# Score matmuls moved from 32x32 to 64x32 array tiles, and a new order of all pieces, in a one-core attention and feed-forward kernel

## The chip, the cores and the metric

The kernel runs on one core of one Trainium2 chip. A core has five engines that run their own instruction queues in order and meet at semaphores: TensorE (PE in the profile, with its weight loads on a row of their own, PEld), VectorE (DVE), ScalarE (ACT), GpSimd (POOL) and SyncE (SP), which only issues DMAs. The metric is device time in microseconds. Three runs of the kernel before gave a median of 218.65 us (218.47 to 218.85).

## The reference, cut to what matters

Inputs are x, 8 batches by 8 heads by 512 tokens by 64, and state, 8 by 8 by 32 by 64. Each head reads both ways; the heads are then joined and go through a two-layer network.

```python
scores = scale * np.matmul(x, state.transpose(0, 1, 3, 2))      # 512 x 32 a head
a = softmax(scores);   xread = np.matmul(a, state)              # 512 x 64
scores2 = scale * np.matmul(state, x.transpose(0, 1, 3, 2))     # the same products, turned
a2 = softmax(scores2); sread = np.matmul(a2, x)                 # 32 x 64
h = concat([xread, sread], tokens), heads side by side          # 8 * 544 rows of 512
r = np.maximum(h @ w_in, 0.0)                                   # 512 -> 2048
out = (s * r * r + b) @ w_out                                   # 2048 -> 512
```

## The kernel before, in words

The whole program is a list of named pieces, ORDER (L15). The loop at L724 takes it word by word and emits each piece's instructions, so ORDER fixes the order in every engine's queue, DMA issues included. It says nothing about how pieces of different engines line up in time: that is left to the semaphores. A piece on another engine, or a load, starts as soon as its own queue and its data allow. The first number in a name is the batch, and a last letter A, V or G puts the piece on ACT, DVE or POOL.

For one batch b the pieces are, in the order of the data:

- x.b (L177) loads x, converted to fp16, by two DMAs that POOL issues. From batch 3 on, POOL first makes a tiny copy that waits for the transposed x of the batch before. xn.b (L188) loads x in another layout by four POOL DMAs; it has two buffers. For batch 0 there are x0.0 and x0.1 and two copies castx.
- xT.b (DVE, L286) transposes x in 32x32 blocks. casts, pair and turn prepare the states: pair.i0.i1 (L255) block-transposes the states i0 to i1 of 16 on DVE, and turn (L243) transposes them on PE, four or fewer at a time, and copies them to the tile stT.
- T.b (PE, L294) makes the scores of all 8 heads: for each of two halves e of the 64 features, four positions hp and two groups g, one matmul of 32 rows by 32 columns of weights and 512 moving columns, 16 in all. U, mu, D, E1, z, At and A (DVE, ACT, POOL) are the softmax over the states, and A holds its result for PE. keep.b (ACT, L309) copies the scores out of PSUM for batches 0, 1, 2 and 7.
- nm, nms, E2, a2, aps, a2T are the other softmax, V.b.c (PE, L403) the read by it for two batches at a time, srd.b (ACT, L423) its copy to srdT.
- M.b.j (PE, L426) multiplies the states by a quarter of w_in: 8 matmuls in tiles of 64 rows by 32 columns. Mc.b.j copies the result to fp16. So xread @ w_in is formed as A @ (state @ w_in), with 256 instead of 512 rows to sum over.
- l.b.f (L378) is that product for one of 16 blocks of 128 features of the first layer: 2 matmuls on PE, a relu on ACT. s.b.f.n squares n blocks. Batches 0 to 2 then use L.b.rr.q (L401), 4 matmuls of the second layer each, and out (DVE) with stores from SP; lh and sh are half-width forms for batch 0. Batches 3 to 7 use seven products in place of eight: S forms sums of blocks, P.b.u is half a product (8 matmuls), ev (L600) evicts a PSUM bank on DVE, and put stores. wsum forms the matching sums of w_out.
- lsr, ssr, S_sr, P_sr, ev_sr do the same for the 256 rows of sread at the end.
- idle.n (L668) issues n matmuls on ones.

PSUM tiles have few buffers: own=1 pieces of T and M share one (tag pt), own=0 pieces share another (pa), l and lh have two (ph), L, P and idle have two (po). A piece that takes a buffer waits for the last reader of the piece that had it.

The 16 matmuls of T run at array positions (row 32 r, column 32 hp) with r = hp ^ g (L300). M uses rows 64 g, and V all 128 rows with 64 columns. All three share that heads of a group stand in the order r = hp ^ g in the column blocks.

Of the kernel before, what the change touches and what calls it, by code (L numbers as in the profile page):

```python
# [78 lines left out]
def kernel(  # L79
# [21 lines left out]
    P = 128  # L101
# [116 lines left out]
    nc.scalar.dma_start(sb_one[:, 0:1], moe_s.unsqueeze(0))  # L218
    nc.scalar.dma_start(sb_one[:, 1:2], moe_b.unsqueeze(0))
    nc.vector.memset(ones16, 1.0)  # L220
    nc.vector.memset(ones32, 1.0)
    xh_t[0] = xpool.tile([P, NG, NT, D], FP16, name="xh_0", tag="xh")

    def load_first_x(g):
# [533 lines left out]
```

## Time and profile before

| what | value |
|---|---|
| median of 3 runs | 218.65 us |
| the profiled execution itself | 218.68 us, span 216.8 us |
| PE busy | 207.0 us, 1920 matmuls |
| DVE busy | 169.4 us |
| ACT busy | 154.7 us |
| POOL busy | 105.0 us |
| granted TensorE clock, mean | 0.998 |

The span is the time from the first to the last instruction of the program; 1.9 us of the execution lie outside it. Busy shares are averages: matmuls overlap, so the start of one piece to the start of the next is the better measure of what a piece costs PE, and it is the one used below. On other engines an instruction's time overlaps a little with the one behind it: relus of 0.60 us follow each other every 0.50 us. In the timeline a row is a run of like instructions with its start, the time from its first start to its last end, and in brackets what the engine waited for.

### The profile page before, as it was taken

The numbers are of one execution on the slowest core, as the hardware profiler recorded it, in microseconds if no ns is written. First come the engines' busy times: TensorE is split into PE (matmuls) and PEld (weight loads), VectorE is DVE, ScalarE is ACT, GpSimd is POOL, SyncE is SP. The second block draws the span as 40 slices with busy tenths as digits, with TensorE's granted clock in tenths as the row PEclk, the third lists the DMA queues.
The fourth block names the chain that finished last, engine by engine and source line by source line (L and its number), as shares of the span: only waits on it lengthen the run. The fifth ranks groups of instructions, "written<-read, shape, count | busy, mean of one in ns | idle before, by whom it ended". The sixth has DMA issues, their size and how long they took to land.

```text
span 216.8 us, 4729 instructions
## 1 busy us (share of the span) xinstructions
PE 207.0 (95%) x1920; PEld 126.4 (58%) x1920; DVE 169.4 (78%) x236; ACT 154.7 (71%) x262; POOL 105.0 (48%) x102
## 2 busy tenths in 40 slices
PE   7668999999999999999999999999999999999992
PEld 2334444344444434545677666776667777888881
DVE  2699885989867879986998799979887964785571
ACT  4378987898858788899889899667668866444400
POOL 8529123494679930525254318836564334225330
PEclk9999999999999999999999999999999999999999
DMA  6999992759497262192908850718903600450055
GB/s 153 186 205 205 199 197 42 125 124 133 106 173 120 48 99 49 38 155 55 144 9 137 139 110 4 97 39 139 205 10 65 131 0 3 87 111 0 0 153 141
DMA packets 23657, 22.42 MB, mean 103 GB/s; under 512 B 4436, under 2 KB 17492, under 8 KB 23636
## 3 DMA queue, kind: packets, MB, share of 16 engines
q0 software_dynamic: 16848, 12.52, 40.8%
q1 hardware_dynamic: 5504, 8.66, 16.4%
q10 hardware_dynamic: 1284, 0.95, 1.6%
q8 instruction: 15, 0.25, 0.5%
q14 instruction: 6, 0.05, 0.1%
HBM read 25.72 MB, written 8.91 MB: 160 GB/s over the span
## 4 chain that ended last, share of the span: by engine, by line
PE 90%; ACT 5%; DMA 2%; DVE 0%; issue 0%; SPq 0%
PE hps L461 24%; PE ops L505 19%; PE opf_X L137 16%; PE opf_W L137 8%; PE mps L137 4%; PE opf_Y L137 4%; PE hps_sr L461 3%; PE vps L137 2%; DMA xf<-in_x_dram 2%; ACT M L152 2%; PE aps L137 2%; PE ops_sr_X L137 2%; PE T_None L137 2%; ACT rh L491 1%; PE dps L672 1%; PE hph L137 1%
## 5 line engine op out<-in xcount | busy, mean ns | idle before, releaser
L465 ACT ACTIVATE r<-hps 128x512 f16<-128x512 f32 x120 | 67.5, 602 | 27.8 <-PE hps L461 26.3
L461 PE MATMUL hps<-A,M 128*128 128x512 f16 x240 | 64.7, 380 | 0.0
L137 PEld LDWEIGHTS <-g 128*128 128x128 f16 x480 | 46.6, 98 | 11.4 <-issue 0.7
L505 PE MATMUL ops<-w_out,g 128*128 128x512 f16 x192 | 46.3, 379 | 0.0
L471 POOL TENSOR_TENSOR g<-r 128x1024 f16<-128x1024 f16 (+1 forms) x14 | 30.4, 2180 | 23.7 <-ACT r L465 23.7
L461 PEld LDWEIGHTS <-M 128*128 128x128 f16 x240 | 21.7, 98 | 22.7 <-issue 6.2
L505 PEld LDWEIGHTS <-g 128*128 128x128 f16 x192 | 18.7, 98 | 22.2 <-issue 0.4
L152 ACT CAST M<-mps 128x1024 f16<-128x1024 f32 x22 | 22.3, 1017 | 1.6 <-PE mps L137 1.5
L469 ACT ACTIVATE g<-r 128x1024 f16<-128x1024 f16 (+1 forms) x18 | 21.4, 1210 | 0.1
L192 POOL DMA_DIRECT2D xn<-in_x_dram x32 | 18.6, 592 | 5.6 <-PE vps L137 4.9
L346 POOL TENSOR_TENSOR At<-E,rz 128x1024 f16<-128x1024 f16 x5 | 9.8, 1964 | 22.0 <-ACT r L465 11.3
L137 PE MATMUL opf_X<-w_T,g 128*128 128x256 f16 x160 | 19.8, 272 | 0.0
L575 DVE TENSOR_TENSOR g<-g 128x1024 f16<-128x1024 f16 (+1 forms) x20 | 17.9, 908 | 1.1 <-POOL S L575 0.9
L575 POOL TENSOR_TENSOR g<-g 128x1024 f16<-128x1024 f16 x4 | 8.8, 2207 | 19.6 <-PE opf_X L137 12.4
L471 DVE TENSOR_TENSOR g<-r 128x1024 f16<-128x1024 f16 (+1 forms) x18 | 14.7, 836 | 1.6 <-ACT r L465 1.6
L152 DVE CAST M<-mps 128x1024 f16<-128x1024 f32 x10 | 12.1, 1213 | 3.5 <-PE mps L137 3.0
L604 DVE SCALAR_TENSOR_TENSOR osx<-opf_X,sb_bc,bias_bc 128x512 f32<-128x512 f32 x15 | 11.2, 746 | 4.0 <-PE opf_X L137 3.9
L292 DVE STREAM_TRANSPOSE xT<-xh 128x1024 f32<-128x1024 f32 (+2 forms) x12 | 10.4, 869 | 4.7 <-ACT xh L152 4.1
L325 POOL TENSOR_TENSOR Dm<-U,mu 128x1024 f32<-128x1024 f32 x3 | 5.7, 1913 | 15.0 <-DVE mu L321 15.0
L465 ACT ACTIVATE r_sr<-hps_sr 128x256 f16<-128x256 f32 x16 | 6.1, 382 | 7.9 <-PE hps_sr L461 7.2
L137 PE MATMUL mps<-w_in,stT 64*32 64x512 f16 x256 | 11.2, 383 | 0.3
L515 DVE SCALAR_TENSOR_TENSOR osb<-ops,sb_bc,bias_bc 128x512 f32<-128x512 f32 x12 | 8.8, 737 | 3.4 <-PE ops L505 3.4
(101 smaller groups left out, 324.3 us busy)
## 6 DMA issues: line engine op xcount, KB each, us to landing
out_dram<-osx SPq DMA_DIRECT2D x36, 128.0 KB, 2.4
xn<-in_x_dram POOLq DMA_DIRECT2D x32, 128.0 KB, 5.1
xh<-in_x_dram POOLq DMA_DIRECT2D x14, 256.0 KB, 5.1
w_in<-in_moe_w_in_dram POOLq DMA_DIRECT2D x8, 256.0 KB, 8.3
w_out<-in_moe_w_out_dram POOLq DMA_DIRECT2D x4, 512.0 KB, 11.2
out_dram<-osb SPq DMA_DIRECT2D x16, 128.0 KB, 2.6
out_dram<-osb SPq DMA_DIRECT2D x16, 64.0 KB, 4.4
xf<-in_x_dram SPq DMA_DIRECT2D x2, 256.0 KB, 3.7
```

The lines of the kernel that those rows point to most:

```text
L137: return nc.tensor.matmul(out, lhsT, rhs, start=start, stop=stop, tile_position=tp, is_transpose=is_transpose, skip_group_check=skip,)
L152: (engine.copy if engine is nc.scalar else engine.tensor_copy)(out, in_)
L192: nc.gpsimd.dma_start(out=xn_t[b][32 * jh : 32 * jh + 32].rearrange("t h c d -> t h (c d)"), in_=x[b].rearrange("h (t jh c) d -> jh t h (c ...
L292: nc.vector.transpose(part(out, p, g), part(in_, p, g))
L346: e.tensor_tensor(out, E1, over_n(rz), ALU.mult)
L461: nc.tensor.matmul(hps, lhsT, rhs, start=(i == 0), stop=(i == len(terms) - 1))
L465: nc.scalar.activation(R_t[tag, q][:, i], hps, AF.Relu)
L469: nc.scalar.activation(g, r, AF.Square)
L471: e.tensor_mul(g, r, r)
L505: nc.tensor.matmul(ops_t[tag, rr], G_t[tag][:, f, P * rr : P * rr + P], w_out_f(f), start=(f == 0), stop=(f == NKF - 1),)
L575: e.tensor_tensor(out, x, y, op)
L604: nc.vector.scalar_tensor_tensor(out, fast(b, name[0]), s_bc, out if plus else bias, ALU.mult, ALU.add)
```

## The change

The scores are now computed in tiles of 64 rows by 32 columns. Each matmul sees the transposed x of two heads at once. For that the transposed states are stored twice, in stZ[0] and stZ[1], with the rows of every other head set to zero: pair first transposes into stZ[0], then multiplies it on DVE by a column of zeros and ones, own, into stZ[1] and, in place, into stZ[0]. The column own is set by five memsets at the start. The count of matmuls stays 16 a batch. The order of heads becomes r = hp ^ 2g in T, V and M alike.

ORDER is new as a whole. It has the same pieces but for these: idle.12, idle.12 and idle.5 become idle.12, idle.11 and idle.4; many squares, sums and copies change engine or are split otherwise; and places differ, of POOL's loads too, in which x.2 now stands behind two squares on POOL. SP's stores keep their kinds, and the last two stores of batch 7 stand between the two of sread.

```diff
 ORDER = [
-    "x0.1 x0.0 castx.1.A xT.0.1.0 casts.A idle.12 pair.0.4 castx.0.A xT.0.0.0 T.0.1.0 U.0.0 turn.0.4.A "
-    "mu.0.0 D.0.V.0 E1.0.0 sb idle.12 keep.0.0 xT.0.1.1 win.0 M.1.0.0 M.0.0.1 x.1 z.0.0 xT.0.0.1 At.0.V.0 "
-    "A.0.0 win.1 wout.0 T.0.0.1 U.0.1 Mc.1.0.A mu.0.1 D.0.V.1 Mc.0.0.A lh.0.2.0 xT.1.1 lh.0.0.0 keep.0.1 "
-    "xT.1.0 idle.5 E1.0.1 win.2 M.0.1.0 T.1.1 sh.0.0.0.V Mc.0.1.A z.0.1 At.0.V.1 A.0.1 lh.0.6.0 lh.0.4.0 "
-    "keep.1 sh.0.6.0.V sh.0.4.0.V sh.0.2.0.G L.0.1.0 lh.0.0.1 lh.0.4.1 lh.0.2.1 M.0.2.0 Mc.0.2.A lh.0.6.1 "
...
-    "l.1.0 l.1.5 pair.4.16 xT.2 sh.0.4.1.V x.3 L.0.1.3 l.1.3 turn.4.12.V out.0.0 out.0.1 l.1.1 T.2.1 U.2 "
-    "M.2.3.0 Mc.2.3.A mu.2 D.2.V l.1.9 L.0.3.0 keep.2 l.1.8 l.1.7 xT.3 s.1.8.2.A L.0.2.0 M.2.1.1 "
...
+    "x0.1 idle.12 castx.1.A casts.A pair.0.4 xT.0.1.0 castx.0.A xT.0.0.0 xT.0.1.1 T.0.1.0 turn.0.4.A "
+    "U.0.0 mu.0.0 keep.0.0 x0.0 D.0.V.0 sb E1.0.0 idle.11 z.0.0 At.0.V.0 win.0 M.1.0.0 xT.0.0.1 M.0.0.1 "
+    "x.1 T.0.0.1 A.0.0 Mc.1.0.A Mc.0.0.A lh.0.2.0 U.0.1 mu.0.1 win.1 keep.0.1 wout.0 xT.1.1 win.2 D.0.V.1 "
+    "lh.0.0.0 sh.0.0.0.G win.3 xT.1.0 idle.4 E1.0.1 z.0.1 M.0.1.0 Mc.0.1.A T.1.1 lh.0.6.0 keep.1 lh.0.4.0 "
+    "At.0.V.1 A.0.1 lh.0.4.1 wout.1 sh.0.2.0.V L.0.1.0 lh.0.0.1 lh.0.2.1 M.0.2.1 Mc.0.2.A lh.0.6.1 "
+    "L.0.0.0 l.0.10 l.0.8 M.1.2.1 Mc.1.2.A sh.0.6.0.V M.0.3.0 l.0.9 l.0.11 M.1.1.1 U.1 mu.1 D.1.V wout.2 "
+    "Mc.0.3.V E1.1 M.1.3.0 sh.0.4.0.G Mc.1.3.V wout.3 l.0.12 l.0.15 L.0.0.1 s.0.10.2.A L.0.1.1 z.1 At.1.V "
+    "st l.0.14 l.0.13 s.0.8.2.G L.0.0.2 Mc.1.1.A L.0.1.2 A.1 s.0.14.2.V s.0.12.2.A sh.0.4.1.G l.1.2 "
+    "l.1.11 cps.0 cps.1 cps.2 cps.3 sh.0.2.1.V sh.0.0.1.V l.1.5 c l.1.10 L.0.0.3 pair.4.16 bias l.1.1 "
+    "l.1.6 L.0.1.3 x.2 xT.2 out.0.1 l.1.9 turn.4.12.V",
+    "l.1.0 s.1.0.2.V T.2.1 keep.2 M.2.3.0 Mc.2.3.A l.1.7 l.1.3 s.1.2.2.A L.0.3.0 sh.0.6.1.V U.2 L.0.3.1 "
...
+    "L.0.2.1 L.0.2.2 l.1.15 l.1.4 s.1.4.2.G M.2.0.0 Mc.2.1.V z.2 At.2.V A.2 T.3.1 U.3 s.1.8.4.A Mc.2.0.A "
+    "l.1.12 L.0.3.3 out.0.3 l.2.4 nm.3 L.0.2.3 L.1.0.0 out.0.2 nms.3.A mu.3 l.2.7 l.2.15 E2.3.0 s.1.6.2.G "
...
+    "l.7.0 S.6.4.0.V put.5.1.1 S.6.4.1.V P.6.6 l.7.8 s.7.6.2.V P.6.7 a2.1 l.7.14 l.7.3 aps.1 a2T.1.A "
+    "ev.6.X2 P.6.8 s.7.12.4.A ev.6.W1 P.6.9 l.7.10 l.7.11 P.6.10 ev.6.X3 s.7.10.2.V V.7.1 srd.7 srd.1 "
+    "l.7.9 s.7.8.2.V P.6.12 lsr.1",
...
 ]
...
-    stE = konst.tile([P, NR, Ns, 2], FP16, name="stE")
+    stZ = [konst.tile([P, NR, Ns, 2], FP16, name=f"stZ_{k}") for k in range(2)]
+    own = konst.tile([P, 2], FP32, name="own")
...
+    nc.vector.memset(own, 0.0)
+    for r in range(4):
+        nc.vector.memset(own[Ns * r : Ns * r + Ns, r % 2 : r % 2 + 1], 1.0)
...
     def pair_states(i0, i1):
         nc.vector.transpose(
-            stE[:, i0:i1].rearrange("p i n e -> p (i n e)").bitcast(FP32),
+            stZ[0][:, i0:i1].rearrange("p i n e -> p (i n e)").bitcast(FP32),
             stn[:, i0:i1].rearrange("p i d -> p (i d)").bitcast(FP32),
         )
+        for k in (1, 0):
+            nc.vector.tensor_scalar(stZ[k][:, i0:i1], stZ[0][:, i0:i1], own[:, k : k + 1], None, ALU.mult)
...
                 for g in range(NG):
-                    r = hp ^ g
+                    r = hp ^ 2 * g
+                    rows = slice(64 * (r // 2), 64 * (r // 2) + 64)
                     mm(
                         part(T[Ns * hp : Ns * hp + Ns], p, g)[:, 0, :],
-                        stE[32 * r : 32 * r + 32, NG * b + g, :, e],
-                        part(at[b]["xT"][32 * r : 32 * r + 32, :, :, e], p, g)[:, 0, :],
+                        stZ[r % 2][rows, NG * b + g, :, e],
+                        part(at[b]["xT"][rows, :, :, e], p, g)[:, 0, :],
                         start=(e == 0), stop=(e == 1),
-                        tp=(32 * r, Ns * hp),
+                        tp=(64 * (r // 2), Ns * hp),
                     )
...
-                    hp = k ^ g
+                    hp = k ^ 2 * g
...
-                r = hp ^ g
+                r = hp ^ 2 * g
```

95 rows, old and new, of the table ORDER are left out of this document.

## The prediction

> **What bounds the kernel now.** I read the page first, then the chain that ended last, then PE's timeline, piece by piece. From the page:
>
> ```profile
> span 216.8 us, 4729 instructions
> PE 207.0 (95%) x1920; PEld 126.4 (58%) x1920; DVE 169.4 (78%) x236; ACT 154.7 (71%) x262; POOL 105.0 (48%) x102
> PE   7668999999999999999999999999999999999992
> PE 90%; ACT 5%; DMA 2%; DVE 0%; issue 0%; SPq 0%
> ```
>
> PE is the bound from the fifth slice on (each is 5.4 us). I laid the starts of PE's pieces against the usual step of their kind (0.43 us for l, 0.86 for L, 0.87 for P). After 25.8 us nothing exceeds it by more than 0.01 us, but for one thing: ahead of every group of tiled matmuls a piece is 0.09 us longer, and the last piece of the group is about 0.11 longer. So behind 26 us the kernel has no waits to win back, only that 0.2 us at each change of tiling. It can lose, wherever the new order makes PE wait. Two stretches of PE's timeline show a change of tiling:
>
> ```profile
> 48.80 0.59 PE L461 MATMUL hps<-A,M 128*128 128x512 f16 x2
> 49.33 0.64 PE L137 MATMUL T_None<-xT,stE 32*32 32x512 f16 x16
> 49.90 0.41 PE L137 MATMUL mps<-w_in,stT 64*32 64x512 f16 x8
> ...
> 63.53 0.62 PE L137 MATMUL mps<-w_in,stT 64*32 64x512 f16 x16
> 64.09 0.39 PE L461 MATMUL hps<-A,M 128*128 128x512 f16 x1
> ```
>
> The reader is to see: T (16 matmuls of 32x32 tiles) takes 49.33 to 49.90 = 0.57 us though M of another tiling follows at once; M behind it takes to 50.25 (where the next piece starts), 0.35. Two pieces of M, 16 matmuls in one tiling, take 63.53 to 64.09 = 0.56; the second starts 0.22 or 0.23 after the first, and then 0.33 to its end. So 8 matmuls in 8 tiles cost 0.226 inside a group and 0.33 as its end.
>
> The start is another matter. This is the chain over it:
>
> ```profile
> 8.25 2.70 PE dps L672 x12
> 10.95 0.39 PE mps L137 x8
> 11.36 1.94 ACT M L152 x2
> ...
> 15.08 0.49 ACT Ts L313
> 15.56 0.04 issue
> 15.61 0.50 PE mps L137 x8
> 16.10 0.02 issue
> 16.13 1.02 ACT M L152
> 17.15 0.05 issue
> 17.19 0.62 PE hph L137 x4
> 17.82 0.02 issue
> 17.84 1.09 ACT rh L491 x2
> 18.93 0.74 ACT Ts L313
> ```
>
> Here ACT sets the pace, with PE's filler matmuls ahead. Two loads stand close behind: w_in's second quarter was issued at 4.85 and 5.53 and landed 9.3 and 10.1 us later, the last at 15.63, just as M.0.1.0 starts (15.61); the fourth quarter, issued at 15.93 and 16.6, landed by 23.8, and M.0.3.0 starts at 24.08.
>
> **Changes of tiling (PE).** T.2 and T.5 stand ahead of an M piece in the new order, T.3 and T.6 behind one, T.4 and T.7 alone; the old order pairs the same pieces. If the 16 matmuls of T fill eight 64x32 tiles like two M pieces, T inside a group costs 2 x 0.226 = 0.45 and a pair 0.45 + 0.33 = 0.78, where the trace has 0.57 + 0.35 = 0.92: -0.13 each. Alone it is 0.56 against 0.575: -0.02. T.3, T.5, T.6: -0.39; T.4, T.7: -0.04; T.2 is counted below. The old T already has four row tiles writing one bank and runs eight wide (16 in 0.57), so I take the new one to run eight wide too. Ends: no faster than M (0.56 for 16), and at worst 0.43 more each, if the two row halves cannot write one bank together (M never asks that: each half writes its own bank).
>
> The Trainium skill's page TensorEngine Tiling (Array Packing), section Restrictions and Gotchas, says that different row tiles cannot access one PSUM bank at a time. The trace of before speaks against it: by that rule the old T, with four row tiles in each bank, would take about four times 0.43 us, and 16 took 0.57. By the rule the sum would end as in the first rival.
>
> **Extra DVE work.** Five memsets lie in DVE's idle 3.0 us before its first transpose. Two multiplications of 128x256 and two of 128x768 are new. Nearest row: the 128x512 multiplication by a column in a2 took 0.363 us. In proportion 0.2 and 0.5 each; the upper bound, from the 128x512 product in At at 0.67, is 0.34 and 1.0. The first pair lies before 6.28, where DVE waits for castx.0: pair.0.4 from 4.87 ends at 5.55 (upper 5.8), xT.0.1.0 then takes 0.45, and xT.0.0.0 still starts at 6.28. Nothing, with 0.0 to 0.3 us of cover left. The second pair stands ahead of bias and xT.2. Its cost is in the next part.
>
> **The start, walked through the new queues with the old rows.** Idle.11 in place of 12 lets M.1.0.0 start at 10.66, 0.22 earlier (its weights landed at 10.56). M.0.1.0 gives that back: its load lands at 15.63. xT.1.1 now stands ahead of D.0.1, so E1.0.1 starts at 15.5 and Mc.0.1 at 16.15 (old 16.13). Behind it ACT's order changes: relu 17.86, keep.1 18.35, two relus from 19.27 and 19.77, then 20.53, 21.03, Mc.0.2 at 21.53 (old 21.71), relus 22.44, 23.24, 23.75, Mc.1.2 at 24.24 (old 24.50). U.1 must be through before M.0.2.1; it now follows two squares and keep.1 and ends at 20.65, before PE wants it (20.85). So -0.26 at this point. POOL issues w_in's last quarter 0.8 us later, behind a square that waits for a later relu, w_out's last quarter 2.5 us and st 2.5 us later; all queue behind transfers that land at 21.2 (w_in), 29.06 (w_out) and 31.55, so I cost that at nothing. If w_in's last quarter lands as much later as it is issued later, M.0.3.0 starts at 24.6, and the 0.26 turns into a loss of 0.5.
>
> At 31 to 38 us x.2 matters: issued at 20.75 before, at about 29.0 now, behind s.0.8.2.G and sh.0.4.1.G. Before it landed at 34.0 and 35.5, behind w_out and st; x's loads took 3.7 to 14.0 us, median 5.2. From its second issue at 29.6 that median gives 34.8. DVE wants it after c (33.95), pair (0.57 + 2 x 0.5, to 35.45) and bias (36.1): xT.2 ends at 37.3, T.2.1 starts at 37.86 (old 38.15). Out.0.1 and turn follow on DVE to 38.35, so M.2.3.0 starts at 38.4, held by 0.1, old 38.73: -0.33, T.2's gain included. At DVE's upper bound xT.2 ends at 38.4 and the gain is lost: +0.6.
>
> **The rest.** The same count of matmuls in the same kinds follows. Waits that I find with no cover: L.1.0.0 behind out.0.3 (U.3 now stands ahead of it on DVE) and P.5.4 behind ev.5.X1 (now behind z.7), both within 0.1 us of holding PE; +0.1 together. And the sread: V.7.1 was 4.7 us ahead of the first lsr, now l.7.9 and P.6.12 alone (1.3 us) are between them, while ACT makes two copies srd, which took 0.73 us each here, about 0.63 apart: +0.17. xn.1 is issued behind S.6.2.1.G at about 172 to 175; xn took at most 6.9 us, and V.7.1 needs it at 182: nothing. DVE, ACT and POOL have, by the rows of their pieces, about +1.5, -5 and +8 us in all, and POOL has room (48%). The last stores: SP's put of batch 7 stands between the two of sread and is issued 0.6 us before the last: nothing, at most 0.6 if SP is late.
>
> **Sum.** 218.68 (span 216.8 + 1.9 around it, 0.03 above the median) - 0.33 - 0.39 - 0.04 + 0.17 + 0.1 = 218.2.
>
> **Rivals.**
> *Row halves take turns in a bank.* In each pass the first four positions write bank by half, the second four the other way round, so every pass falls in two: +0.43 us for each of six T on a busy PE: 218.2 + 2.6 = 220.8. Against: the old T. For: no row has 64-row tiles sharing a bank.
> *x.2 lands late.* For: it is issued 8 us later, and in the busy stretch w_in's loads took 8.3 us in the median. Then it lands at 37.9, xT.2 ends at 39.1, T.2.1 is held by 1.3 us: 219.5. It is slower than before from a landing after 37.1 on, by over 0.2% after 37.6. Against: it waited only for what lies ahead of it.
> *The start gives nothing and re-ordered producers hold PE here and there.* DVE's margins at many evictions are 0.1 to 0.8 us by my walk, over stretches of DVE work with an error of a few tenths. Without the -0.33 and with three holds of 0.2: 219.1.
> *The tiling does not save.* The cost at a change may lie with leaving the full array alone; then T saves nothing: 218.2 + 0.5 = 218.7.
>
> **Chances.** Forecast 0.47 (own range 217.8 to 218.6); bank 0.07; late load 0.10; scattered holds 0.24; no saving 0.12. I call within 0.2% (0.44 us) no change, about what a measurement here can tell. Faster is the forecast's better side and little else: 0.42. Within: its other part, no saving, half of the scattered holds: 0.31. Slower: 0.27. The range 217.7 to 219.6 leaves out the bank and a tail of the holds.
>
> **What would show it.** T rows 64*32 with x16 and the next M piece 0.45 us behind (right), or 0.9 (bank). M.2.3.0 at 38.4; DVE idle before xT.2 for the load xh would mean a late load. A gap of 0.2 us ahead of the first hps_sr matmul. No PE step more than 0.1 us over its kind elsewhere; any such step names the producer that I mis-timed. The prediction is wrong if PE waits over 0.5 us in any one place after 26 us, or if M.0.3.0 starts after 24.1.

## The result, and the profile after

The changed kernel takes 221.22 us (median of 4 runs, 220.9 to 221.63) against 218.65: a ratio of 1.0112, 95% interval 1.0095 to 1.0129. The forecast was 218.2 in a range of 217.7 to 219.6. It was wrong in sign and outside its range.

The profiled execution is one of 220.9 us with a span of 218.4, against 218.68 and 216.8. Its page, the lines that answer to those of before:

```profile
span 218.4 us, 4742 instructions
PE 208.0 (95%) x1918; PEld 126.0 (58%) x1918; DVE 172.2 (79%) x250; ACT 151.0 (69%) x255; POOL 117.2 (54%) x105
PE   7868999999999999999999999999999999998992
PE 76%; DMA 9%; DVE 6%; POOL 2%; ACT 2%; issue 2%; SPq 1%; DVEq 0%; ACTq 0%; POOLq 0%
```

The first lines of such a page hide the loss: PE's busy share is the same 95%. The last line shows it. The chain that ended last was 90% PE before; now it is 76%, and DMA and DVE carry 15%, so PE waits for loads or stores somewhere. Part of that is the start, where the order is new; part lies behind 26 us, where there was nothing but PE before.

Laid against the usual step of their kind, PE's pieces between 36 us and the last product give this account:

| place | us |
|---|---|
| M.2.3.0 starts at 38.47 instead of 38.73 | -0.26 |
| changes of tiling, T.3 to T.7 | -0.36 |
| L.0.3.3 and L.0.2.3 longer by 0.17 and 0.46 | +0.62 |
| V.7.1 and P.6.12 longer by 0.08 and 0.15 | +0.23 |
| lsr.14 and lsr.15 longer by 0.86 and 0.44 | +1.29 |
| sum | +1.52 |
| P_sr.6 starts at 213.10 instead of 211.62 | +1.48 |
| from there to the end of the execution, 7.80 instead of 7.06 | +0.74 |

So 1.48 + 0.74 = 2.22 = 220.9 - 218.68; 0.04 is left between the pieces.

**The tiles.** PE's timeline over T.3:

```profile
47.77 0.41 PE L137 MATMUL mps<-w_in,stT 64*32 64x512 f16 x8
47.99 0.63 PE L137 MATMUL T_None<-xT,stZ 64*32 64x512 f16 x16
48.56 0.60 PE L468 MATMUL hps<-A,M 128*128 128x512 f16 x2
...
51.79 1.02 PE L512 MATMUL ops<-w_out,g 128*128 128x512 f16 x4 [0.29 <-DVE osb L522]
```

M and T now share a tiling: T starts 0.22 behind M and takes 0.57 as the end of the group. T.2 and T.5, which stand ahead of M, take 0.464. A pair of T and M so takes 0.79 where it took 0.92: 0.12 less for T.3, T.5 and T.6, and nothing for T.4 and T.7, which stand alone. The last line is L.1.0.0, which the profile shows as held by DVE; more on it below.

**The largest loss.** The chain over 189 to 199 us, in order of time:

```profile
188.40 0.89 PE opf_W L137 x8
189.31 0.76 DVE osx L611
190.09 0.53 SPq L620
...
191.65 0.58 SPq L620
192.28 3.68 DMA out_dram<-osx
196.24 0.57 issue
197.14 0.55 DVE g L582
198.69 0.60 PE hps_sr L468 x4
```

It leaves PE at 189.3 and comes back at 198.7. P.6.11 (188.40) completes bank W of batch 6; ev.6.W2 evicts it into osx (189.31); SP issues the stores of that tile (190.09 to 192.2); the last lands 3.7 us later, at 196.0; and only then DVE goes on. DVE's and ACT's timelines say who waits:

```profile
189.31 0.75 DVE L611 SCALAR_TENSOR_TENSOR osx<-opf_W,sb_bc,osx 128x512 f32<-128x512 f32 x1 [0.99 <-PE opf_W L137]
192.58 2.01 DVE L582 TENSOR_TENSOR g<-g 128x2048 f16<-128x2048 f16 x2
196.14 0.75 DVE L611 SCALAR_TENSOR_TENSOR osx<-opf_X,sb_bc,bias_bc 128x512 f32<-128x512 f32 x1 [1.55 <-DMA out_dram<-osx]
196.81 0.42 DVE L478 TENSOR_TENSOR g_sr<-r_sr 128x512 f16<-128x512 f16 x1
```

```profile
198.26 0.66 ACT L472 ACTIVATE r_sr<-hps_sr 128x256 f16<-128x256 f32 x2 [2.02 <-DVE g_sr L478]
```

The eviction at 196.14 is ev.7.X1, the first of batch 7. It writes the same tile osx, of which there is one buffer, so it waits for the store of the batch before. It holds DVE for 1.55 us, and the squares ssr behind it start late. They are the readers of r_sr, so ACT's relus of the sread find no buffer (2.02), and PE's lsr matmuls find no PSUM. In the kernel before, ev.6.W2 was done at 185.94 and ev.7.X1 started at 193.48, 7.5 us later, with no wait for a store (the 2.04 us of the last line come up again further down):

```profile
185.19 0.75 DVE L604 SCALAR_TENSOR_TENSOR osx<-opf_W,sb_bc,osx 128x512 f32<-128x512 f32 x1
...
193.48 0.75 DVE L604 SCALAR_TENSOR_TENSOR osx<-opf_X,sb_bc,bias_bc 128x512 f32<-128x512 f32 x1 [0.63 <-PE opf_X L137]
194.15 2.04 DVE L575 TENSOR_TENSOR g<-g 128x1024 f16<-128x1024 f16 x1
```

From the eviction's end to the last landing its stores took 4.6 us; now they took 5.9, and in the new order ev.7.X1 is ready 4.5 us behind the eviction.

The 1.3 us between 4.6 and 5.9 are one late store. Of the four stores of that tile the first three land 2.3 to 2.5 us behind their issue, the fourth 3.68; in the kernel before all four take 2.3 to 2.4. In the trace a 16 KB packet of an instruction queue runs from 193.67 to 194.81, within the fourth store's time, and the slowest of the store's own packets start one behind another from 194.81 on, as it ends. In the four profiles, here and below, in which these stores follow lsr.7, the fourth takes 3.4 to 4.1 us with such a packet in its time; in the nine others it takes 2.4, with none. With the usual 4.6 us ev.7.X1 would have waited about 0.25 us, not 1.55 (an estimate from these numbers). So the new place took away 3 us of margin and put the last store beside that packet.

**The second loss.** DVE's timeline, and POOL's, around the load of x.3, and the chain through it ("issue" is time for which the profile shows no cause):

```profile
44.00 1.25 DVE L298 STREAM_TRANSPOSE xT<-xh 128x1024 f32<-128x1024 f32 x1 [1.07 <-DMA xh<-in_x_dram]
...
49.89 1.21 DVE L324 STREAM_TRANSPOSE U<-T_None 128x1024 f32<-128x1024 f32 x1
51.02 0.71 DVE L522 SCALAR_TENSOR_TENSOR osb<-ops,sb_bc,bias_bc 128x512 f32<-128x512 f32 x1
```

```profile
37.23 0.17 POOL L181 COPY ahead<-xT 1x2 f16<-1x2 f16 x1 [7.32 <-DVE xT L298]
37.46 1.06 POOL L184 DMA_DIRECT2D xh<-in_x_dram  x2
```

```profile
37.98 5.49 DMA xh<-in_x_dram
43.47 0.03 issue
43.50 0.05 DVEq L298
43.55 0.45 issue
44.00 1.25 DVE xT L298
```

The tiny copy ahead of x.3 waits for xT.2, so x.3 is issued at 37.46 and 37.98, and its second half lands at 43.47. DVE sees that at 43.55 and starts xT.3 only at 44.00. In all, xT.3 (44.00) starts 1.07 after DVE was free for it; all of DVE behind it, A.2, U.3 and out.0.3, is that much later, and out.0.3 (51.02) frees the PSUM buffer that L.1.0.0 needs. DVE had about 0.5 us of margin there, not 1.07. The 0.45 us between the end of the wait and xT.3 stand in all eight profiles with the new tiles in which DVE waits for x.3; in the three with the old tiles (the kernel before among them) they are 0.04 to 0.05. Why is open.

### The profile page after: what moved, and what is told of

Its sections match the earlier page's. It is cut to its first block, busy times and chain, and to the rows that moved or that the text cites. A ratio compares the mean times of both kernels' runs of the same rounds, so it can differ in the third digit from the quotient of the medians.

```text
span 218.4 us, 4742 instructions
## 1 busy us (share of the span) xinstructions
PE 208.0 (95%) x1918; PEld 126.0 (58%) x1918; DVE 172.2 (79%) x250; ACT 151.0 (69%) x255; POOL 117.2 (54%) x105
## 4 chain that ended last, share of the span: by engine, by line
PE 76%; DMA 9%; DVE 6%; POOL 2%; ACT 2%; issue 2%; SPq 1%; DVEq 0%; ACTq 0%; POOLq 0%
PE hps L468 21%; PE ops L512 15%; PE opf_X L137 15%; PE opf_W L137 8%; DMA w_in<-in_moe_w_in_dram 5%; PE mps L137 3%; PE opf_Y L137 3%; DMA xh<-in_x_dram 3%; PE vps L137 2%; DMA out_dram<-osx 2%; PE aps L137 2%; PE ops_sr_X L137 2%; PE hps_sr L468 2%; PE hph L137 1%; DVE xT L298 1%
## 5 line engine op out<-in xcount | busy, mean ns | idle before, releaser
L468 PE MATMUL hps<-A,M 128*128 128x512 f16 x240 | 65.9, 380 | 0.0
L478 POOL TENSOR_TENSOR g<-r 128x1024 f16<-128x1024 f16 (+1 forms) x8 | 21.5, 2690 | 17.8 <-ACT r L472 17.8
L582 POOL TENSOR_TENSOR g<-g 128x1024 f16<-128x1024 f16 (+1 forms) x9 | 22.8, 2530 | 9.3 <-PE hps L468 4.0
L152 ACT CAST M<-mps 128x1024 f16<-128x1024 f32 x26 | 26.6, 1041 | 1.2 <-PE mps L137 1.2
L478 DVE TENSOR_TENSOR g<-r 128x1024 f16<-128x1024 f16 (+1 forms) x25 | 22.6, 919 | 4.8 <-ACT r L472 4.8
L476 ACT ACTIVATE g<-r 128x1024 f16<-128x1024 f16 (+1 forms) x13 | 18.1, 1395 | 0.1
L332 POOL TENSOR_TENSOR Dm<-U,mu 128x1024 f32<-128x1024 f32 x4 | 9.5, 2364 | 11.4 <-DVE mu L328 8.4
L582 DVE TENSOR_TENSOR g<-g 128x1024 f16<-128x1024 f16 (+1 forms) x17 | 14.8, 883 | 0.1
L353 POOL TENSOR_TENSOR At<-E,rz 128x1024 f16<-128x1024 f16 x3 | 5.7, 1913 | 14.5 <-DVE rz L344 8.1
L641 POOL TENSOR_TENSOR g_sr<-g_sr 128x512 f16<-128x512 f16 (+1 forms) x3 | 4.4, 1477 | 14.1 <-DVE g_sr L478 9.4
```

The lines of the kernel that those rows point to most:

```text
L152: (engine.copy if engine is nc.scalar else engine.tensor_copy)(out, in_)
L332: e.tensor_tensor(blk(part(Dm, p)), blk(part(at[b]["U"], p)), over_n(part(at[b]["mu"], p)), ALU.subtract)
L468: nc.tensor.matmul(hps, lhsT, rhs, start=(i == 0), stop=(i == len(terms) - 1))
L476: nc.scalar.activation(g, r, AF.Square)
L478: e.tensor_mul(g, r, r)
L582: e.tensor_tensor(out, x, y, op)
```

## Experiments

Executions of the new order fall into two groups some 5 to 7 us apart, with a few in between, by a mechanism that the second experiment shows; ratios are those of the lower group, where both occur. "The kernel before" was run beside each: 218.81 and 218.63 us (29 runs each) on the chips of the first eight kernels, 218.88 (35 runs) on that of the last four.

### The tiles alone

The changed code with the order of before.

```diff
 # after.py
-ORDER = [ ... order of after.py ... ]
+ORDER = [ ... order of before.py ... ]
```

> The new score tiles and the doubled states, in the old order of pieces. Theory 1 (the loss comes from the order: three places where PE is held, 0.53 us at 49 to 52, 0.23 at V.7.1, 1.29 at 195 to 199, while the tiles save 0.1 to 0.13 for each T): the two multiplications stand before xT.2 in the old order, so T.2.1 starts about 0.6 later than 38.15, and the T pieces give back 0.5: 218.4 to 219.1. Rival (the doubled states or the tiles themselves cost, in PE or outside the span): 220.5 to 221.5.

Measured: 219.91 us (219.1 to 220.8, 12 runs), ratio 1.0052 (1.0031 to 1.0073). Slower, not faster. The expected hold at T.2.1 is there, but it sets off another. DVE's and PE's lines, with T.2.1 at 38.76 and l.2.6 at 52.43:

```profile
36.67 0.88 DVE L265 TENSOR_SCALAR stZ<-stZ,own 128x768 f16<-128x768 f16 x2
```

```profile
38.76 0.65 PE L137 MATMUL T_None<-xT,stZ 64*32 64x512 f16 x16 [0.52 <-DVE xT L298]
...
52.43 1.04 PE L468 MATMUL hps<-A,M 128*128 128x512 f16 x4 [1.52 <-DVE A L363]
```

The two multiplications take 0.88 us and delay xT.2 by as much. The copy ahead of x.3 waits for xT.2, so x.3 is issued at 39.0 instead of 38.05; xT.3 starts at 46.43 instead of 43.96, A.2 at 51.66, and PE waits 1.52 at l.2.6. Of the 2.47 us, 0.95 are the later issue, 0.41 the idle stretch behind the wait that comes with the new tiles, and the rest a second half of x.3 that took 6.3 us instead of 5.2. T.5 and T.6 save their 0.12 each, as expected, but one late DVE step costs a second time through the load that waits for it.

### The order alone

The code of before with the new order.

```diff
 # before.py
-ORDER = [ ... order of before.py ... ]
+ORDER = [ ... order of after.py ... ]
```

> The new order of pieces with the old 32x32 tiles and single states. Theory 1: all three holds stay, and the T pieces are 0.4 to 0.5 dearer than in the changed kernel: 221.2 to 221.8. Rival (tiles or doubled states cost): near 218.7 to 219.5.

Measured: 225.58 us (224.3 to 225.76, 6 runs), ratio 1.0293 (1.0265 to 1.0322). The expectation was three holds and 221.2 to 221.8. The hold at lsr.14 and lsr.15 is there (1.24 + 0.44), and so is that at P.6.12 (0.16): they belong to the order. The hold at L.0.3.3 and L.0.2.3 is not there: both take their usual step to 0.001 us. x.3 was issued 0.09 us earlier than in the changed kernel, landed at 43.37, and xT.3 started at 43.49, so out.0.3 was 0.51 earlier; most of that is the 0.41 of idle time that only the new tiles have. PE, with its dearer T, also came to L.1.0.0 0.16 us later. So the order alone does not make this hold. And 3.5 us more were lost at l.5.12. DVE's, POOL's and PE's timelines around it:

```profile
134.75 4.62 DVE L575 TENSOR_TENSOR g<-g 128x2048 f16<-128x2048 f16 x1
139.29 0.74 DVE L604 SCALAR_TENSOR_TENSOR osx<-opf_X,sb_bc,bias_bc 128x512 f32<-128x512 f32 x1
```

```profile
134.64 3.65 POOL L471 TENSOR_TENSOR g<-r 128x2048 f16<-128x2048 f16 x1 [3.29 <-ACT r L465]
```

```profile
140.09 1.86 PE L137 MATMUL opf_X<-w_T,S 128*128 128x256 f16 x8 [3.31 <-DVE osx L604]
```

The same two instructions in the changed kernel:

```profile
134.58 1.21 DVE L582 TENSOR_TENSOR g<-g 128x2048 f16<-128x2048 f16 x1
```

```profile
134.86 4.39 POOL L478 TENSOR_TENSOR g<-r 128x2048 f16<-128x2048 f16 x1 [3.68 <-ACT r L472]
```

DVE's sum S.4.4.2 and POOL's square s.5.0.4 become ready within 0.3 us of each other, and one of them is stopped until the other is done. Where DVE starts first (134.58), its sum takes 1.21 and POOL's square 4.39 instead of 3.65, which nobody waits for. Where POOL starts first (134.64), DVE's sum takes 4.62: 134.64 + 3.65 = 138.29, and 138.29 + 1.1 is its end, 139.37. Behind it stands ev.4.X2, and PE waits for the bank. A race of 0.1 to 0.3 us so decides over 3.5 us. After the hole PE ran below full clock: the windows of this execution give 0.50 and 0.84 in place of 1.00.

```profile
140.00:141.80 1.80, 1.71 (x9) 1.19 (x9) 1.80 (x4) 0.00 (x0) 0.00 (x0) 0.50 0.00 0
141.80:146.30 4.50, 4.50 (x31) 3.12 (x30) 3.10 (x4) 1.39 (x4) 0.00 (x0) 0.84 0.00 0
```

(The clock is the third number from the end. The second is a mean: the trace has 0.50 from 139.79 to 143.20, 3.41 us, and 1.00 behind it.) P.4.8, l.5.15 and P.4.9 are longer by 0.79, 0.42 and 0.30 there, so the lost race costs 5.0 us in all. This is the upper group.

### The store of batch 6 left out

The changed kernel without the stores of half i = 0 of batch 6, put.6.0.0 and put.6.0.1. Those rows of the output stay unwritten.

```diff
     def put(b, i, rr):
+        if (b, i) == (6, 0):
+            return
```

> The changed kernel without the four stores of the first half of batch 6 (put.6.0.0 and put.6.0.1), so that part of the output stays unwritten. Theory: ev.7.X1 waits for these stores to land, because the tile osx_0 has one buffer; without them it starts at about 192.8 in place of 196.1, lsr.14 and lsr.15 lose their gaps of 0.86 and 0.44, and the time falls by 1.3 to 219.6 to 220.2. Rival (the relu of lsr.14 waits for the squares ssr.0 and ssr.2 on DVE, which stand behind S.7.4.0 and P.7.2 anyway): a gap of 0.5 or more stays at lsr.15, and the time falls by 0.3 to 0.8 only.

Measured: six runs of 218.87 to 220.66 us, two of 222.21 and 222.78, and two of 224.89 and 225.31; ratio of the six 1.001 (0.9983 to 1.0037). Their median, 219.01, is below the range that was expected. The profile is that of the run of 220.66, in which all of PE is 1.8 to 1.9 us late from the start on. In it lsr.14 and lsr.15 take their usual step to 0.001 us, while the holds at L.0.2.3 (0.45) and P.6.12 (0.15) stay. So the wait for the store is shown: without the store there is no hold, and the rival, squares that come late by themselves, has fallen.

### The eviction of batch 6 earlier

P.6.11 and ev.6.W2 ahead of the sread instead of behind lsr.7; nothing is left out.

```diff
-    ... V.7.1 srd.7 srd.1 l.7.9 s.7.8.2.V P.6.12 lsr.1 lsr.0 P.6.13 lsr.10 ev.6.X4 s.7.0.4.G lsr.7 P.6.11 ev.6.W2 lsr.5
+    ... V.7.1 P.6.11 srd.7 srd.1 ev.6.W2 l.7.9 s.7.8.2.V P.6.12 lsr.1 lsr.0 P.6.13 lsr.10 ev.6.X4 s.7.0.4.G lsr.7 lsr.5
```

> The changed kernel with P.6.11 moved up to right behind V.7.1, and its eviction ev.6.W2 ahead of the square s.7.8. The stores of batch 6's first half start about 4 us earlier, and srd.7 and srd.1 get 0.87 us more cover. Theory: the gaps of 1.29 us at lsr.14 and lsr.15 and of 0.23 at V.7.1 and P.6.12 both go: 219.5 to 220.0. If only the copies srd were at fault: 221.0; if only the store: 219.9.

Measured: four runs of 219.62 to 220.97, one of 223.04 and five of 225.08 to 226.14; ratio of the four 1.0055 (1.0029 to 1.0081). The holds at P.6.12, lsr.14 and lsr.15 are gone, with the 0.08 at V.7.1, and a new one of 0.26 stands at lsr.7. The race was lost in the profiled execution (POOL 134.73, DVE 134.82 for 4.62 us), with 3.46 at l.5.12.

### The changed kernel again

Unaltered, beside the three that follow.

> The changed kernel itself, unaltered, on the chip of the next three, to set them against. As measured so far: 220.9 to 221.7. If the square s.5.0 on POOL (3.6 us) and the sum S.4.4 on DVE meet in the other order here, as in two of the runs before, where S.4.4 took 4.62 us in place of 1.2: 224 to 226 in a part of the executions.

Measured: 220.42, 220.47, 220.54 and 226.3, 227.04, 227.27 us; ratio of the lower 1.0077 (1.005 to 1.0104). The two groups are in the changed kernel itself; its first four runs were all of the lower. The profiled one has the same holds as the first profile: 0.57 at L.0.3.3 and L.0.2.3, 0.15 at P.6.12, 1.03 at lsr.14 and lsr.15. The 0.08 at V.7.1 is not there: that piece takes its usual step in every profile but the first. POOL's square shows a start 0.03 us ahead of DVE's sum here (134.68 and 134.71), and the sum took 1.21 all the same; a lead that small in the profile's start times does not tell who comes first.

### x.3 without its wait

```diff
-        if b > 2:
+        if b > 3:
```

This is the condition of the tiny copy in load_x. xh has two buffers, and that of batch 1 is free for batch 3 once xT.1 is done, so x.3 need not wait for xT.2.

> The changed kernel, in which the load x.3 no longer waits for xT.2: it is issued right behind x.2, at about 30 in place of 37.5. Theory: xT.3 starts at 42.9 without waiting (44.0 in the changed kernel), A.2 and out.0.3 end a microsecond earlier, and the gaps of 0.07 at L.0.3.3 and 0.46 at L.0.2.3 go: 0.5 less than the changed kernel. Rival (DVE's own work, with U.3 ahead of out.0.3, holds L.1.0.0): the gap at L.0.2.3 stays at 0.3 or more.

Measured: lower group 219.59 to 220.37 (4 of 10 runs), ratio 1.0053 (1.0026 to 1.0079). Its DVE and POOL:

```profile
42.73 1.24 DVE L298 STREAM_TRANSPOSE xT<-xh 128x1024 f32<-128x1024 f32 x1
50.11 0.71 DVE L522 SCALAR_TENSOR_TENSOR osb<-ops,sb_bc,bias_bc 128x512 f32<-128x512 f32 x1
```

```profile
28.62 2.23 POOL L184 DMA_DIRECT2D xh<-in_x_dram  x4
```

x.2 and x.3 are issued together at 28.62, xT.3 follows the eviction before it without a wait, out.0.3 is 0.91 earlier (0.1 of it from the start), and both holds are 0.000. P_sr.6 starts at 212.09, 0.49 ahead of the run above. So the wait for x.3 is shown as the cause of both holds. It says nothing of why the wait ends 0.45 us before xT.3 starts, which with the order alone it did not.

### The tiles, with the states prepared one step earlier

The tiles with the old order, pair.4.16 moved ahead of bias.

```diff
-    ... c bias l.1.0 l.1.5 pair.4.16 xT.2
+    ... c pair.4.16 bias l.1.0 l.1.5 xT.2
```

> The new tiles and doubled states in the old order, with one word moved: pair.4.16 ahead of bias, into the 1.3 us that DVE waits there. Theory (what the tiles alone cost, 1.1 us, is the delay of xT.2 by the two multiplications, and through it of x.3, of xT.3 and of A.2): xT.2 ends at 37.7 as in the kernel before, no gap at M.2.0.0, and T.2, T.3, T.5 and T.6 each save 0.11 to 0.13: 0.3 to 0.6 under the kernel before. Rival (the tiles or doubled states cost elsewhere): 0.3 to 1.1 over it.

Measured: 219.81 us (219.33 to 220.25, 10 runs), ratio 1.0045 (1.0028 to 1.0062). Not faster: the same collision, in another place.

```profile
35.01 2.49 DVE L262 TENSOR_SCALAR stZ<-stZ,own 128x768 f16<-128x768 f16 x2
```

```profile
34.93 1.89 POOL L475 TENSOR_TENSOR g<-r 128x1024 f16<-128x1024 f16 x1 [6.12 <-ACT r L469]
```

The multiplications that took 0.88 us in the run of the tiles alone take 2.49 beside a square of POOL that started 0.08 earlier: 1.81 to the end of that square, then 0.68. xT.2 is later than before, and the cascade through x.3 returns.

### Early eviction, and the colliding square on ACT

```diff
 # order as in "the eviction of batch 6 earlier", and
-    s.5.0.4.G
+    s.5.0.4.A
```

> The changed kernel with P.6.11 early, as in the last set, and the square s.5.0 moved from POOL to ACT. Theory (what made the runs with P.6.11 early fall apart into 219.6 to 221 and 223 to 226 is that S.4.4 on DVE waits for the whole of s.5.0 on POOL when POOL starts first, by 0.1 us): all executions in the lower group, 219.5 to 220.2, S.4.4 at 1.2 us. Rival (the upper group has another cause, such as loads or stores): both groups stay.

Measured: 219.64 us; eleven of 12 runs lie between 218.93 and 219.88, one at 221.74; ratio 1.0041 (1.002 to 1.0063). With POOL out of the race the upper group is gone (the one run at 221.74 is far from it, and its cause is open), where the unaltered kernel on the same chip had three of six in it. The holds left are L.0.2.3 (0.45), lsr.7 (0.26) and l.6.0 (0.10). DVE at ev.7.X1, the second line:

```profile
192.85 2.01 DVE L579 TENSOR_TENSOR g<-g 128x2048 f16<-128x2048 f16 x2
194.78 0.74 DVE L608 SCALAR_TENSOR_TENSOR osx<-opf_X,sb_bc,bias_bc 128x512 f32<-128x512 f32 x1
```

It follows the sums with no idle time; the store has landed by then.

### All three repairs

```diff
 # order as above, and
-        if b > 2:
+        if b > 3:
```

> The changed kernel with three repairs: x.3 loaded without waiting for xT.2, P.6.11 and ev.6.W2 ahead of the sread (so that the store of batch 6 lands before ev.7.X1 needs its tile), and the square s.5.0.4 on ACT instead of POOL. Theory (late x.3 0.5 us, store wait 1.3 us, collision of POOL and DVE, and they add up): about 0.5 us under the run without the repair of x.3 (219.64), so 219.1 to 219.3, all executions in one group; no piece of PE held at L.0.3.3, L.0.2.3, l.5.12, lsr.14 or lsr.15, and P_sr.6 starts at 211.6, like in the kernel before. Rival (each hold hides another one that comes up when the first is gone): 219.6 or more, with new held pieces between 50 and 200 us.

Measured: 218.97 us (218.56 to 219.86, 12 runs, one group), ratio 1.0005 (0.9988 to 1.0022). P_sr.6 starts at 211.55, like before (211.62). The repairs add up; the holds at lsr.7 (0.26) and l.6.0 (0.10) stay. So the loss of the changed kernel is explained to within what a measurement tells: it lies in the wait for the store and the copies for sread, which the order brings by itself, and in the wait for x.3, which the order alone does not bring: it held PE only in kernels with the new tiles.

### The tiles with the states prepared in an idle stretch

The tiles with the old order, pair.4.16 ahead of the bias column c.

```diff
-    ... L.0.0.3 c bias l.1.0 l.1.5 pair.4.16 xT.2
+    ... L.0.0.3 pair.4.16 c bias l.1.0 l.1.5 xT.2
```

> The 64x32 tiles with the old order, but the transposition of the states of batches 2 to 7 and its two multiplications moved ahead of the bias column c, into DVE's idle stretch (the states land at about 32.6 us, POOL is idle until 34.6). Theory: they take 0.57 + 0.88 us there, c ends at 34.8, bps is not late (35.04), xT.2 starts at 36.1 instead of 36.55, T.2.1 is not held and x.3 is issued no later than before. Then only the saving at the changes of tiling is left: 0.35 us for T.3 to T.7 and 0.1 for T.2, so 0.3 to 0.5 us under the kernel before (218.2 to 218.4). Rival (the tiles cost something that the old order does not show, or the saving is lost in the tail): 218.6 or more. Second rival: the states land so late that the multiplications run into POOL's square at 34.6 and take 2.5 us as they did one step later: c and bias late, 219.8.

Measured: 218.46 us (217.63 to 219.35, 12 runs) beside 218.88, ratio 0.998 (0.9964 to 0.9997): 0.42 us faster than the kernel before. DVE, POOL and PE:

```profile
31.89 0.58 DVE L257 STREAM_TRANSPOSE stZ<-stn 128x384 f32<-128x384 f32 x1
32.51 0.88 DVE L262 TENSOR_SCALAR stZ<-stZ,own 128x768 f16<-128x768 f16 x2
33.30 0.75 DVE L665 TENSOR_SCALAR c<-cps,sb_bc 128x512 f16<-128x512 f32 x1
...
35.61 1.23 DVE L295 STREAM_TRANSPOSE xT<-xh 128x1024 f32<-128x1024 f32 x1
```

```profile
34.16 1.89 POOL L475 TENSOR_TENSOR g<-r 128x1024 f16<-128x1024 f16 x1 [6.16 <-ACT r L469]
```

```profile
37.71 0.65 PE L134 MATMUL T_None<-xT,stZ 64*32 64x512 f16 x16
38.17 0.40 PE L134 MATMUL mps<-w_in,stT 64*32 64x512 f16 x8
```

The multiplications take 0.88 and are through 0.8 us before POOL's square starts. c ends at 34.05, bps waits for nothing, xT.2 starts at once behind bias, and T.2.1 has no idle time ahead of it. From T.2.1 to the start of P.7.13 it is 167.73 us, against 168.23 in the profile of before: 0.50, nearly all of it four groups that save 0.12 each; T.4 and T.7 save nothing. This is what the tiles are worth, and this version has the lowest median measured here. The new order with its three repairs is 0.51 us behind it: about 0.36 are the two holds left there, and 0.2 the time outside the span (below).

### The order of the last stores

From P_sr.6 to the end of the execution the changed kernel took 0.74 us more, most of it outside the span. The changed kernel with the three repairs and the last store of batch 7 back in its old place, and the kernel before with that store in its new place:

```diff
 # the three repairs
-    ev_sr.1.1.X.1.1 put.7.1.1
+    put.7.1.1 ev_sr.1.1.X.1.1
```

```diff
 # before.py
-    put.7.1.1 ev_sr.1.1.X.1.1
+    ev_sr.1.1.X.1.1 put.7.1.1
```

> The changed kernel with the three repairs and, in addition, the last store of batch 7 placed ahead of the eviction and store of the first sread half, as in the kernel before. Theory A (the 0.3 to 0.6 us that the changed kernel spends more outside the span come from the order of the last stores): 0.3 to 0.6 us under the run with the three repairs alone, 218.6 to 218.9. Theory B (they do not): within 0.2 us of that run.

> The kernel before, with only the last store of batch 7 moved behind the eviction and store of the first sread half, as in the changed kernel. Theory A (the order of the last stores costs time outside the span): 0.3 to 0.6 us over the kernel before, 219.0 to 219.2. Theory B: no change, 218.5 to 218.8.

Measured: 218.98 us (218.55 to 219.59) with the three repairs, where 218.97 was without the move; and 219.36 (218.86 to 219.72) for the kernel before with the store moved, ratio 1.0024 (1.001 to 1.0039). The first speaks for theory B. The second has the sum of theory A but not its place: its time outside the span is 1.94 us in the median, that of before is 1.96; the span grew, from 216.9 to 217.45. So the order of the last stores does not set the time outside the span in either kernel. That it costs 0.5 us inside the span of one and nothing in the other is measured and not explained.

The time outside the span, execution less span, median over the executions of each kernel:

| kernels | us |
|---|---|
| old order: before, tiles alone, the two with pair moved, the last store moved | 1.87 to 1.97 |
| new order: order alone, store left out, and the three with the square on ACT | 2.11 to 2.16 |
| new order: after, after again, early eviction, x.3 early | 2.37 to 2.46 |

It goes with the order, 0.2 to 0.5 us more in the new one. Among the kernels of the new order, the four in the last row, and only they, show an 8 KB packet of an instruction queue behind the end of the span (at 220.66 in the changed kernel); those of the old order show it as well, at 1.9 us outside. What sets it stays open.

## Why the prediction was wrong, by its own steps

- **Changes of tiling: right.** Inside a group T takes 0.464 (0.45 said), as its end 0.565, M ahead of it 0.227. T.3 to T.7 save 0.36 (0.43 said; T.4 and T.7 save nothing). With the states prepared in an idle stretch it is a measured 0.42 us.
- **The rival of the bank: fallen.** Two row halves of 64 write one bank in T.2, each its own partitions of it, and 16 matmuls took 0.464; taking turns would be some 0.43 more. The rule of the Trainium skill's page TensorEngine Tiling (Array Packing), section Restrictions and Gotchas, that different row tiles cannot access one bank at a time, does not hold here, with 32-row tiles before or 64-row tiles after.
- **The start: right in its steps, not clear as a gain.** Mc.0.1 at 16.17 (16.15 said), Mc.0.2 at 21.60 (21.53), Mc.1.2 at 24.30 (24.24), T.2.1 at 38.00 (37.86), M.2.3.0 at 38.47 (38.4). M.0.3.0 started at 23.92, so w_in's last quarter was not late. The second pair of multiplications took 0.88 (1.0 said). The rival of a late x.2 did not come. But M.2.3.0 is at 38.54 in another profile of the old order (the last store moved) and at 38.34 to 38.77 in six others of the new one, one late start left out, so the 0.26 is no more than what two profiles differ by.
- **"Waits that I find with no cover ... +0.1 together": this is the step that failed.** The list misses one wait and mis-sizes another, and PE lost 1.91 us by the two. The one that it misses: ev.7.X1 writes the tile osx, which has one buffer, so it waits for the landing of batch 6's stores. The new place of P.6.11 and ev.6.W2, behind lsr.7, put 4.5 us between where the stores needed 5.9, and 4.6 even at their usual length. That is +1.29 in the profile; leaving the store out and evicting earlier both end the hold. The other: L.1.0.0 behind out.0.3 was named, but as a matter of 0.1; it is 0.62 with the piece before it. There the walk stopped at x.2. x.3 is tied to xT.2 by the copy ahead of it, was issued at 37.46, and xT.3 started 1.07 us after DVE was free for it, 0.45 of that behind the end of the wait and not explained. P.5.4 was held by 0.01.
- **The sread, +0.17: right.** P.6.12 is held by 0.15, behind the copies srd. The 0.08 at V.7.1 is a pause in the middle of that piece, ahead of the copies, and comes in this profile alone.
- **"The last stores ... nothing, at most 0.6 if SP is late": mis-sized, and not for that reason.** From P_sr.6 to the end it took 0.74 more, 0.6 of it outside the span. The time outside the span does not follow the order of the last stores, as the last pair of runs shows; what sets it stays open. The term asks only when the last stores are issued. The stores of batch 6, for which ev.7.X1 waits, are in no term of the prediction.
- **"POOL has room (48%)": wrong as a reading.** The share says nothing of what POOL does to DVE. The profile of before showed it: a sum on DVE took 2.04 us there from 194.15 where it usually takes 0.69, while POOL worked on a sum until 195.64. I read past it. In this kernel it makes the upper group, 5 to 7 us higher; the lower group, on which the ratio above rests, is not touched by it.
- **The rivals.** Held producers were the right kind and the wrong size: three holds of 0.2 were put at 0.6 us together, and there are 2.14 in three places. The time outside the span, 0.6 of the 2.2 us (2.46 in the profiled execution, 1.87 before), is in none of them. That the tiling would not save has fallen with the first point.

The sum with its terms as measured is 218.68 - 0.26 - 0.36 + 0.62 + 0.23 + 1.29 - 0.04 + 0.74 = 220.9.

## What to carry to other kernels

When the order of a kernel changes, walk every buffer with one copy from its last reader to its next writer, stores to DRAM included: the four stores of a tile took 4.6 to 6.3 us from the eviction to the last landing here, and the engine that waits for it stops everything behind it. Do the same for each load that is tied to a step of the load before. And look for pairs of a large VectorE operation on SBUF and a GpSimd operation that become ready together: the sums, squares and multiplications seen here did not overlap, and which one waits can be a matter of 0.1 us.

## What the runs showed of the hardware

**VectorE and GpSimd shut each other out.** A DVE sum of two fp16 tiles (128x2048) takes 1.21 us when it comes first and 4.62 beside a POOL square that started 0.11 us before it; that square takes 3.65 when it comes first and 4.39 behind a DVE sum that started 0.28 before it. Two DVE multiplications by a column (128x768 fp16) take 0.88 alone and 2.49 beside POOL. In each case the second ends its own length or a little less behind the end of the first (1.08 for the sum, 3.46 for the square, 0.68 for the multiplications), so it is a lock and not a share. The Trainium skill's page SBUF — State Buffer, section SBUF: two separate sides, says just that: VectorE operations in a two-port mode, or with two SBUF inputs beside a GpSimd operation that reads SBUF, contend with GpSimd for a shared port pair that is held for a whole instruction. The traces here agree, with the numbers above; whether the multiplications, which read one tile, were in a two-port mode no run here shows. What I had not expected is that such a race gives one kernel two times, 220.5 and 226 to 227 us, with nothing else changed; with the square on ACT the upper group was gone.

**A hole costs clock.** After PE had idled for 3.3 us in the kernel with the order alone, the granted clock was 0.50 for 3.41 us (139.79 to 143.20) and 1.00 behind it, and three pieces took 1.5 us more.

**A store beside an instruction packet.** A 16 KB packet of an instruction queue took 1.14 us (193.67 to 194.81) in the changed kernel and 1.50 us (198.38 to 199.88) with the order alone, and the store that it fell into landed 3.68 and 4.07 us behind its issue instead of 2.4. The fourth store was late in each of the four profiles in which the two met, and in none of the others; that the packet is the cause is argued from these times, as no run moved the packet alone.
